# A planner that counts TensorE's products and keeps SyncE's transposes clear of instruction fetches

## The chip, the cores and the metric

The kernel runs on one core of one Trainium2 chip. The metric is the device time of one execution in microseconds (us); three timed executions are shown, and their median counts. One more execution was recorded by the hardware profiler, and has a time of its own.

The engines are called as the profile calls them: PE (TensorE, with PEld for its weight loads), DVE (VectorE), ACT (ScalarE), POOL (GpSimd) and SP (SyncE, which here issues nearly all DMAs). A q behind a name means the engine's sequencer, for instance while it issues a DMA.

## The reference

Two parts follow each other. The first is a linear attention with decay (RWKV6): batch 4, 8 heads, 768 tokens, head size 48.

```python
for t in range(S):
    cur = np.einsum('bhd,bhe->bhde', u[None] * kt, vt)
    y[:, :, t] = np.einsum('bhd,bhde->bhe', rt, state + cur)
    state = wt[:, :, :, None] * state + np.einsum('bhd,bhe->bhde', kt, vt)
...
h = x @ w_in
g = np.maximum(0.01 * h, h)
return g @ w_out
```

The second takes `y` as `x`, 3072 tokens of 384 values, through two dense layers with a leaky ReLU between them: 384 to 2048 and back to 384. Everything comes and goes as float32.

## The kernel before, in words

The 3072 tokens are cut into 24 chunks of 128, six to each batch element. A chunk goes through these steps:

- four loads of `w`, `k`, `r`, `v` into a tile `in` (L634, issued by SP; the first four chunks are loaded in pairs at L444);
- `lw`, the logarithm of the decays (L644, ACT), and its running sum `cum` on TensorE (L650, L653);
- two exponentials (L676, L680, ACT) and two products on DVE that give `rk`, the scaled `r` and `k` (L359);
- the transposed `rkT`. For the first 12 chunks TensorE transposes (L370) and DVE or ACT copies the result out; for chunks 12 to 23 (`RK_DMA = 12`) SP issues a transpose by DMA (L697);
- the scores on TensorE (L721), from chunk 8 on for two chunks in one step, the mask on DVE (L729), the state's sums (L739, L754) and the output `intra` (L765, L770);
- `y` (L432, DVE), with a bonus term that POOL and DVE make (L389 to L401), and its transpose into `xT`: on TensorE (L418) for the first 12 chunks, by DMA (L784) for chunks 12 to 23.

The dense layers run over blocks of one or two chunks: six of one, seven of two, four of one. "Up" multiplies `xT` by `w_in_b` (L828), ACT applies the leaky ReLU and writes `g` (L843), "down" multiplies `g` by `w_out_b` (L857); the result is copied (L868, L870) and stored (L874, SP). At the start TensorE runs 42 products of zeros (L894).

No scheduler orders this. The kernel calls no engine while it describes its work: `step` hands the class `Plan` each step with its possible engines and their costs, a priority, what it depends on, the tiles it reads and takes, and for a DMA a triple `wire` of wire time, size and latency. `Plan.order` then plays the steps through in time: whenever an engine is free, it takes from its ready steps the one with the smallest priority whose tiles are free. Attention steps have priorities of ten times the chunk's number, the dense layers 1000 and more, so the dense products fill TensorE wherever no attention step is ready. The order in which steps began there is the order in which the instructions are then written, for each engine; on the chip each engine works through its own list in order, and waits at a step whose data or tiles are not there.

For a DMA, the plan keeps SP busy for the step's cost, puts the wire time on one shared wire, and holds the data for landed the latency later. The costs for the transposes by DMA:

```python
TRK = (1.75, 64, 1.8)
TY = (0.65, 24, 1.8)
...
s_T = [step(
    {"SP": 0.6},
    lambda e: nc.sync.dma_start_transpose(
        out=rkT.t[:], in_=rk.t[:].rearrange("p a h d -> p (a h d)")),
    P0, deps=[s_r, s_k], reads=[rk], takes=[rkT], wire=TRK, late=0.5)]
```

Of the kernel before, what the change touches and what calls it, by code (L numbers as in the profile page):

```python
# [22 lines left out]
class Plan:  # L23
# [4 lines left out]
    SEEN = {"PE": 0.21, "DVE": 0.05, "ACT": 0.05, "POOL": 0.07, "SP": 0.05}  # L28

    def __init__(self, limits, slack_from, slack):  # L30
        self.steps, self.late, self.limits = [], [], limits
        self.slack_from, self.slack = slack_from, slack

    def add(self, engs, fn, pri, deps=(), reads=(), takes=(), wire=None, late=0.0):
        i = len(self.steps)
        self.late.append(late)
        self.steps.append([engs, fn, pri, {d for d in deps if d is not None}, tuple(reads), tuple(takes), wire])
        for b in (*reads, *takes):
            b.users.append(i)
        return i  # L40

    def order(self, pools):
        n = len(self.steps)
# [5 lines left out]
        bufs = {}  # L49
# [3 lines left out]
        remain = {k: len(b.users) for k, b in bufs.items()}  # L53
        free_tiles = {p: [(0.0, k) for k in range(len(t))] for p, t in pools.items()}
        in_use = {}
        ready_at = [0.0] * n
# [3 lines left out]
        events = []  # L60
        dma_free, flying = 0.0, []

        def offer(i, t):
# [9 lines left out]
        while events:  # L73
            now, kind, e, i = heapq.heappop(events)
# [12 lines left out]
            for e in self.ENGINES:  # L87
# [3 lines left out]
                while ready[e]:  # L91
                    pri, i = heapq.heappop(ready[e])
                    if self.start[i] is not None:
                        continue
                    want, ok = {}, True
                    for b in self.steps[i][5]:
                        if b.t is None:
                            want[b.pool] = want.get(b.pool, 0) + 1
                            if in_use.get(b.kind, 0) >= self.limits.get(b.kind, 99):
                                ok = False  # L100
                    for p, k in want.items():
                        if sum(f <= now + 1e-9 for f, _ in free_tiles[p]) < k:
                            ok = False
                    if ok:
                        chosen = i
                        break
                    held.append((pri, i))
# [16 lines left out]
                out.append(i)  # L124
                count += 1
                free[e] = now + d - (self.OVER[e] if d > 0.3 else 0.0)
                if wire is None:
# [20 lines left out]
        if count != n:  # L148
            raise RuntimeError(("stuck", count, n, [(self.steps[i][0], self.steps[i][2]) for i in range(n) if self.start[i] is None][:20]))
        return out  # L150

# [5 lines left out]
ROWS = (0.6, 8, 1.5)  # L157
TRK = (1.75, 64, 1.8)
TY = (0.65, 24, 1.8)


@with_exitstack
def kernel(
# [90 lines left out]
    with tc.manual_schedule():  # L254
# [55 lines left out]
        def weight_steps(q, which, pri):  # L310
# [13 lines left out]

            ld = step({"SP": 0.5}, load, pri, takes=[st], wire=WEIGHT)
            made = []
# [34 lines left out]
        def transposes(P0, rk, kind, s_d, rkTb, out_of, pri_k=0):  # L361

            tr = Buf("ps", "tr")

            def view(tr=tr):
                return tr.t[:].bitcast(BF16).rearrange("p (g t) -> p g t", t=128)

            def tpose(e):
                for g in range(NP):
                    nc.tensor.transpose(  # L370
                        view()[:, g, :], rk.t[:, kind, 2 * g : 2 * g + 2, :].rearrange("p h d -> p (h d)"), ident[:])

            def evac(e):
                if e == "DVE":
                    nc.vector.tensor_copy(out=out_of(), in_=view()[:, 0:NP, :])
                else:
                    nc.scalar.copy(out=out_of(), in_=view()[:, 0:NP, :])

            s_tr = step({"PE": 0.23}, tpose, P0, deps=[s_d], reads=[rk], takes=[tr])
            return step({"DVE": 0.42, "ACT": 0.59}, evac, P0, deps=[s_tr], reads=[tr], takes=[rkTb])  # L380
# [31 lines left out]
        def to_xt(P0, y, yp, s_ye, col_of):  # L412
            def yT():
                return yp.t[:].bitcast(BF16).rearrange("p (g t) -> p g t", t=128)

            def typose(e):
                for g in range(KT):
                    nc.tensor.transpose(  # L418
                        yT()[:, g, :], y.t[:].rearrange("p h d -> p (h d)")[:, g * 128 : (g + 1) * 128], ident[:])

            def xcopy(e):
                if e == "DVE":
                    nc.vector.tensor_copy(out=col_of(), in_=yT()[:, 0:KT, :])  # L423
                else:
                    nc.scalar.copy(out=col_of(), in_=yT()[:, 0:KT, :])
            s_yt = step({"PE": 0.18}, typose, P0 + 1, deps=[s_ye], reads=[y, yp])
            return step({"ACT": 0.48, "DVE": 0.36}, xcopy, P0 + 1, deps=[s_yt], reads=[yp])
# [9 lines left out]
        def pair(n):  # L437
# [23 lines left out]
            def cum(bank, mats):  # L461
                def go(e):
                    for j in range(2):
                        nc.tensor.matmul(
                            heads(bank.t), lhsT=mats[j][:], rhs=lw.t[:, j, :, 0:D], start=(j == 0), stop=(j == 1),
                            skip_group_check=True)
                return step({"PE": 0.33}, go, P0, deps=[s_ln], reads=[lw], takes=[bank])

# [15 lines left out]

            s_tot = step({"PE": 0.3}, total, P0 + 0.5, deps=[s_ln, s_cg], reads=[lw, cg])
            a_in = Buf("a")
# [41 lines left out]
            for js in range(2):  # L528
# [13 lines left out]

                s_sc = step({"PE": 0.42}, scores, P0 + 1, deps=s_T, reads=[rkT], takes=sc)
                m = Buf("m")
# [13 lines left out]
            def sums(e):  # L558
# [11 lines left out]
                {"PE": 0.4}, sums, P0 + 1, deps=[s_rk[1, 0], s_rk[1, 1], *s_vbs, s_sc],  # L570
                reads=[*rk, *vbs], takes=pp)
            sb, sx = Buf("sb"), Buf("s")
# [17 lines left out]
            def intra(e):  # L590
# [18 lines left out]
            s_y = step(  # L609
                {"PE": 1.2}, intra, P0 + 1, deps=[*s_ms, *s_vbs, *s_T, s_sb], reads=[*ms, *vbs, rkT, sb], takes=yps)  # L610
            for j in range(2):
# [8 lines left out]
        def single(n):  # L620
# [11 lines left out]
            for i, src in enumerate((w, k, r, v)):  # L632
                def load(e, src=src, i=i):
                    nc.sync.dma_start(out=part(i)(), in_=src[b, :, t0 : t0 + L, :].rearrange("h p d -> p h d"))  # L634
                lds.append(step(
                    {"SP": 0.5}, load, P0 + i * 0.1, takes=[slot], wire=LOAD,
                    deps=[firsts[n - AHEAD]] if n - AHEAD in firsts else []))
# [19 lines left out]

            s_cum = firsts[n] = step({"PE": 0.27}, cum, P0, deps=[s_ln], reads=[lw], takes=[cp])
            ci, ek = Buf("ci"), Buf("ps", "ek")
# [34 lines left out]
            else:  # L694
                s_T = [step(
                    {"SP": 0.6},
                    lambda e: nc.sync.dma_start_transpose(  # L697
                        out=rkT.t[:], in_=rk.t[:].rearrange("p a h d -> p (a h d)")),
                    P0, deps=[s_r, s_k], reads=[rk], takes=[rkT], wire=TRK, late=0.5)]
            vs, s_vs = bonus(P0, [slot], rv, kv, vv, ([rl], [kl], [vl]))  # L700
# [33 lines left out]
            if not last:  # L734
# [9 lines left out]

                s_pp = step({"PE": 0.17}, sums, P0 + 2, deps=[s_k, s_vb, s_sb], reads=[rk, vb], takes=[pp])

# [16 lines left out]
            def intra(e):  # L763
# [10 lines left out]
            s_y = step({"PE": 0.38}, intra, P0 + 1, deps=[*s_m, *s_T, s_vb, s_sb],  # L774
                reads=[m, vb, rkT] + ([] if first else [sb]), takes=[yp])
            y = Buf("y")
# [4 lines left out]
            else:  # L781
                xt_steps[n] = [step(
                    {"SP": 0.6},
                    lambda e: nc.sync.dma_start_transpose(  # L784
                        out=xT[:, :, col : col + L], in_=y.t[:].rearrange("p h d -> p (h d)")),
                    P0 + 1, deps=[s_ye], reads=[y], wire=TY, late=0.5)]
            yield
# [3 lines left out]
        for n in range(NCH):  # L791
# [3 lines left out]
            elif n % 2 == 0:  # L795
                two = [single(n), single(n + 1)]
                asked = [next(t) for t in two]
                if n >= JOIN:
                    (d0, t0, c0, f0), (d1, t1, c1, f1) = asked
                    s_sc = [step(  # L800
                        {"PE": 0.65}, lambda e, f0=f0, f1=f1: (f0(e), f1(e)), n * 10 + 1,
                        deps=[*d0, *d1], reads=[t0, t1], takes=[*c0, *c1])] * 2
                else:
                    s_sc = [
                        step({"PE": 0.42}, f, (n + i) * 10 + 1, deps=d, reads=[t], takes=c)
                        for i, (d, t, c, f) in enumerate(asked)]
# [7 lines left out]
        for nb, size in enumerate(blocks):  # L814
# [7 lines left out]
            for j in range(0, NJ, J):  # L822
                hp = Buf("ps", "hp")

                def up(e, hp=hp, j=j, J=J, N=N, c0=c0):
# [9 lines left out]
                s_up = step(  # L835
                    {"PE": J * KT * (N / 2400 + 0.0027)}, up, pri, takes=[hp],
                    deps=[s for ch in chs for s in xt_steps[ch]] + win_s[j * 128 // 512])
# [10 lines left out]
            for ch in chs:  # L848
                off = (ch - chs[0]) * L
                cols = [(0, 256), (256, DM)] if ch == NCH - 1 else [(0, DM)]  # L850
                for c_lo, c_hi in cols:
                    op = Buf("ps", "op")
                    s_dn = None
                    for q in range(4):
                        def down(e, op=op, g=g, q=q, off=off, c_lo=c_lo, c_hi=c_hi):
# [6 lines left out]
                            {"PE": 4 * ((c_hi - c_lo) / 2400 + 0.0025)}, down, pri,  # L862
                            deps=g_done[q * 4 : q * 4 + 4] + wout_s[q] + [s_dn], reads=[g], takes=[op])
                    o = Buf("o")

                    def ocopy(e, o=o, op=op, c_lo=c_lo, c_hi=c_hi):
# [5 lines left out]
                    step(  # L872
                        {"SP": 0.5},
                        lambda e, o=o, ch=ch, c_lo=c_lo, c_hi=c_hi: nc.sync.dma_start(  # L874
# [8 lines left out]
        step({"PE": 0.0}, lambda e: None, 1000.0, deps=[up_first[2]], reads=[warm])  # L883
        order = plan.order(pools)
        global PLAN
# [44 lines left out]
```

## Time and profile before

| what | us |
|---|---|
| timed runs | 183.87, 182.80, 183.69 |
| median | 183.69 |
| the profiled execution, its own time | 182.08 |
| its span, first to last instruction | 180.2 |
| PE busy in the span | 174.7 |
| DVE, ACT, POOL busy | 116.6, 110.7, 99.6 |
| `rkT<-rk` transposes by DMA: 12, median time from issue to landing | 4.1 |
| `xT<-y` transposes by DMA: 12, median time from issue to landing | 3.4 |

The span leaves out what lies around the first and the last instruction, 1.9 us here. Rows of the profile name an engine, a line of the kernel, and the tile written and the tiles read as out<-in. "PEld L828 <- DMA xT<-y: 0.3, 1, 0.3" in the list of waits means that weight loads of line 828 waited 0.3 us in total for a DMA into `xT`, once, 0.3 us at longest. In the DMA part, the queue named "instruction" carries the engines' own instructions, which are fetched while the kernel runs.

### The profile page before, as it was taken

What the parts mean: (1) busy time and instruction counts of PE and PEld (TensorE: products, weight loads), DVE (VectorE), ACT (ScalarE), POOL (GpSimd) and SP (SyncE); (2) the same over time, 40 slices, a digit from 0 to 9 for tenths busy, and PEclk for the clock granted to TensorE, in tenths of its full rate; (3) what the DMA queues carried; (4) which work ended last, traced back from release to release, by engine and by line L of the source; (5) the groups of instructions that cost most, each with busy time, mean ns of one, the idle gap of its engine ahead of it and who ended that gap; (6) DMA issues with size and microseconds to landing.
All of it is one profiled execution on the core that took longest, in us unless ns stands there. A gap on an engine that the chain in (4) does not pass through costs nothing.

```text
span 180.2 us, 5557 instructions
## 1 busy us (share of the span) xinstructions
PE 174.7 (97%) x2208; PEld 134.0 (74%) x2208; DVE 116.6 (65%) x241; ACT 110.7 (61%) x241; POOL 99.6 (55%) x141
## 2 busy tenths in 40 slices
PE   7999999999999999999999999999999999999993
PEld 4457887778778779787777687777687786778882
DVE  4389774369889799989489655686853484441111
ACT  2664868567978889857684168754286762535430
POOL 6297970376987898877837255654482655000000
PEclk9999999999999999999999999999999999999999
DMA  6999999899999999899999898999997992522102
GB/s 149 261 281 347 386 371 347 162 198 244 201 174 214 187 218 195 174 191 203 204 208 225 99 220 174 172 230 224 149 220 164 181 222 58 146 68 66 45 3 87
DMA packets 116524, 34.57 MB, mean 192 GB/s; under 512 B 109713, under 2 KB 114962, under 8 KB 116498
## 3 DMA queue, kind: packets, MB, share of 16 engines
q1 hardware_dynamic: 116496, 34.22, 94.3%
q8 instruction: 17, 0.28, 0.7%
q14 instruction: 9, 0.07, 0.1%
q10 hardware_dynamic: 2, 0.00, 0.0%
HBM read 25.17 MB, written 4.72 MB: 166 GB/s over the span
## 4 chain that ended last, share of the span: by engine, by line
PE 87%; ACT 3%; DMA 3%; DVE 2%; SPq 1%; issue 1%; DVEq 0%; ACTq 0%
PE ps L828 33%; PE ps L857 32%; PE ps L894 4%; PE ps L370 3%; DMA in<-in_w_dram 3%; PE ps L721 2%; PE ps L770 2%; PE ps L650 2%; PE ps L765 2%; PE ps L739 1%; PE ps L597 1%; SPq L634 1%; DVE m L549 1%; ACT g L843 1%; PE ps L418 1%
## 5 line engine op out<-in xcount | busy, mean ns | idle before, releaser
L828 PE MATMUL ps<-xT,w_in_b 128*128 128x128 bf16 (+1 forms) x816 | 75.9, 241 | 0.2
L843 ACT ACTIVATE g<-ps 128x512 bf16<-128x512 f32 x96 | 56.3, 597 | 32.0 <-PE ps L828 26.1
L857 PE MATMUL ps<-w_out_b,g 128*128 128x384 bf16 (+2 forms) x400 | 74.7, 319 | 0.1
L828 PEld LDWEIGHTS <-w_in_b 128*128 128x128 bf16 x816 | 60.0, 98 | 10.1 <-DVE xT L423 0.5
L857 PEld LDWEIGHTS <-g 128*128 128x128 bf16 x400 | 35.5, 97 | 15.8
L389 POOL TENSOR_TENSOR ru<-in,ub 128x384 f32<-128x384 f32 x24 | 24.0, 1000 | 21.0 <-DMA in<-in_k_dram 17.3
L359 DVE TENSOR_TENSOR rk<-in,ps 128x384 bf16<-128x384 f32 x48 | 25.1, 550 | 14.3 <-ACT ps L680 5.9
L393 POOL TENSOR_TENSOR ru<-ru,in 128x384 f32<-128x384 f32 x24 | 24.0, 999 | 8.9 <-DMA in<-in_r_dram 7.9
L729 DVE TENSOR_TENSOR m<-ps,maskb 128x512 bf16<-128x512 f32 x40 | 25.0, 682 | 4.3 <-PE ps L721 4.3
L401 POOL TENSOR_TENSOR vs<-in,dg 128x384 f32<-128x384 f32 x24 | 19.9, 830 | 8.7 <-DVE dg L397 8.6
L868 DVE COPY o<-ps 128x384 f32<-128x384 f32 (+2 forms) x16 | 8.5, 531 | 19.9 <-PE ps L857 14.3
L708 POOL TENSOR_TENSOR sb<-s,a 128x384 bf16<-128x384 f32 x18 | 14.9, 830 | 8.6 <-ACT a L671 8.5
L432 DVE TENSOR_TENSOR y<-ps,vs 128x384 bf16<-128x384 f32 x24 | 13.2, 552 | 5.1 <-PE ps L770 4.7
L397 DVE TENSOR_REDUCE dg<-ru 128x8 f32<-128x384 f32 x24 | 13.0, 547 | 4.0 <-POOL ru L393 4.0
L409 POOL CAST vb<-in 128x384 bf16<-128x384 f32 x24 | 12.0, 506 | 3.1 <-DMA in<-in_v_dram 2.2
L662 DVE TENSOR_TENSOR ci<-ps,lw 128x384 f32<-128x384 f32 x20 | 11.0, 552 | 3.6 <-PE ps L653 3.2
L644 ACT ACTIVATE lw<-in 128x384 bf16<-128x384 f32 x20 | 10.4, 522 | 2.0 <-DMA in<-in_w_dram 2.0
L676 ACT ACTIVATE ps<-ps 128x384 f32<-128x384 f32 x20 | 9.6, 480 | 2.9 <-DVE ci L662 2.6
L671 ACT ACTIVATE a<-ps 64x4 f32<-64x4 f32 x36 | 6.1, 169 | 8.1 <-DVE ci L662 7.0
L894 PE MATMUL ps<-zeros 128*128 128x256 bf16 (+1 forms) x42 | 9.0, 348 | 1.1 <-DVE zeros L257 1.1
L680 ACT ACTIVATE ps<-ci 128x384 f32<-128x384 f32 x20 | 9.8, 491 | 0.0
L754 DVE TENSOR_TENSOR s<-ps,sb 128x384 f32<-128x384 f32 x14 | 7.7, 550 | 2.1 <-PE ps L739 2.0
(78 smaller groups left out, 161.7 us busy)
## 6 DMA issues: line engine op xcount, KB each, us to landing
out_dram<-o SPq DMA_DIRECT2D x23, 192.0 KB, 3.3
in<-in_w_dram SPq DMA_DIRECT2D x20, 192.0 KB, 4.1
in<-in_k_dram SPq DMA_DIRECT2D x20, 192.0 KB, 4.0
in<-in_r_dram SPq DMA_DIRECT2D x20, 192.0 KB, 4.2
in<-in_v_dram SPq DMA_DIRECT2D x20, 192.0 KB, 4.0
in<-in_moe_w_in_dram SPq DMA_DIRECT2D x4, 768.0 KB, 9.5
in<-in_moe_w_out_dram SPq DMA_DIRECT2D x4, 768.0 KB, 12.7
in<-in_w_dram SPq DMA_DIRECT2D x2, 384.0 KB, 5.0
```

The costliest lines, as they stand in the source:

```text
L359: nc.vector.tensor_tensor(out=o, in0=x, in1=i, op=ALU.mult)
L389: lambda e: nc.gpsimd.tensor_tensor(out=ru.t[:], in0=kv(), in1=ubv, op=ALU.mult),
L393: lambda e: nc.gpsimd.tensor_tensor(out=ru.t[:], in0=ru.t[:], in1=rv(), op=ALU.mult),
L397: lambda e: nc.vector.tensor_reduce(out=dg.t[:], in_=ru.t[:], axis=AX.X, op=ALU.add),
L401: lambda e: nc.gpsimd.tensor_tensor(out=vs.t[:], in0=vv(), in1=dg.t[:].unsqueeze(2).to_broadcast([128, H, D]), op=ALU.mult),
L432: lambda e: nc.vector.tensor_tensor(out=y.t[:], in0=heads(yp.t), in1=vs.t[:], op=ALU.add),
L708: lambda e: nc.gpsimd.tensor_tensor(out=sb.t[:].rearrange("p g a d -> p (g a) d"), in0=s_in.t[:].rearrange("p g a d -> p (g a) d"), in1=a_ ...
L729: lambda e, par=par: nc.vector.tensor_tensor(out=m.t[:, par, :, :], in0=sc[par].t[:].rearrange("p (g t) -> p g t", g=NP), in1=maskb[:].uns ...
L828: nc.tensor.matmul(hp.t[:, a * N : (a + 1) * N], lhsT=w_in_b[:, t, (j + a) * 128 : (j + a + 1) * 128], rhs=xT[:, t, c0 : c0 + N], start=(a ...
L843: lambda e, hp=hp, g=g, j=j, J=J, N=N: nc.scalar.activation(out=g.t[:, j : j + J, 0:N], in_=hp.t[:, 0 : J * N].rearrange("p (a n) -> p a n ...
L857: nc.tensor.matmul(op.t[:, c_lo:c_hi], lhsT=g.t[:, j, off : off + 128], rhs=w_out_b[:, j, c_lo:c_hi], start=(j == 0), stop=(j == NJ - 1))
L894: nc.tensor.matmul(warm.t[:, 0:cols].rearrange("p (a n) -> p a n", n=256), lhsT=zeros[:, 0:128], rhs=zeros[:].unsqueeze(1).to_broadcast([1 ...
```

## The change

The planner gets a count of TensorE's products: each step on TensorE says how many it holds (`mm`), and the plan adds them up, starting from 36 for the zero products. It holds that an instruction fetch happens at product 866 and every 126.6 products from there. The order is made three times; from the second time on, the times of the fetches found in the run before are known, and a step marked `xbar` (the two transposes by DMA) may not begin on SP within 4.5 us ahead of a fetch. It is put off until the fetch begins, and SP takes another ready step. Besides, SP's costs are set anew: a load, a weight load and a store 0.57 instead of 0.5 us, a transpose 1.3 and 1.25 instead of 0.6, and the wire times and latencies of the transposes are made shorter. No instruction is added or taken away; the order of the instructions differs.

```diff
+    PIECE, FIRST_PIECE, ZEROS, CLEAR = 126.6, 866.0, 36, (0.0, 4.5)
...
-    def add(self, engs, fn, pri, deps=(), reads=(), takes=(), wire=None, late=0.0):
+        self.mm, self.xbar, self.fetches = [], [], []
+
+    def add(self, engs, fn, pri, deps=(), reads=(), takes=(), wire=None, late=0.0, mm=0, xbar=False):
         i = len(self.steps)
         self.late.append(late)
+        self.mm.append(mm)
+        self.xbar.append(xbar)
...
+        for b in bufs.values():
+            b.t, b.free_at = None, 0.0
...
+        products, piece, fetches = self.ZEROS, self.FIRST_PIECE, []
...
                     want, ok = {}, True
+                    until = max([f - self.CLEAR[0] for f in self.fetches if now < f - self.CLEAR[0] and f < now + self.CLEAR[1]], default=0.0)
+                    if self.xbar[i] and until > now + 1e-9:
+                        ok = False
+                        heapq.heappush(events, (until, 1, "SP", -1))
...
+                if e == "PE":
+                    products += self.mm[i]
+                    if products >= piece:
+                        fetches.append(now + d * (1 - (products - piece) / self.mm[i]))
+                        piece += self.PIECE
...
+        self.fetches = fetches
         return out
...
-TRK = (1.75, 64, 1.8)
-TY = (0.65, 24, 1.8)
+TRK = (1.25, 64, 1.2)
+TY = (0.47, 24, 1.0)
...
-                    {"SP": 0.5}, load, P0 + i * 0.1, takes=[slot], wire=LOAD,
+                    {"SP": 0.57}, load, P0 + i * 0.1, takes=[slot], wire=LOAD,
...
-                    {"SP": 0.6},
+                    {"SP": 1.3},
                     lambda e: nc.sync.dma_start_transpose(
                         out=rkT.t[:], in_=rk.t[:].rearrange("p a h d -> p (a h d)")),
-                    P0, deps=[s_r, s_k], reads=[rk], takes=[rkT], wire=TRK, late=0.5)]
+                    P0, deps=[s_r, s_k], reads=[rk], takes=[rkT], wire=TRK, late=0.5, xbar=True)]
...
-                    {"SP": 0.6},
+                    {"SP": 1.25},
                     lambda e: nc.sync.dma_start_transpose(
                         out=xT[:, :, col : col + L], in_=y.t[:].rearrange("p h d -> p (h d)")),
-                    P0 + 1, deps=[s_ye], reads=[y], wire=TY, late=0.5)]
+                    P0 + 1, deps=[s_ye], reads=[y], wire=TY, late=0.5, xbar=True)]
...
-        order = plan.order(pools)
+        for _ in range(3):
+            order = plan.order(pools)
```

The other places of the diff hand `mm` to each TensorE step, and 0.57 to the weight loads and the stores.

More of the change, by code (lines that the diff above doesn't have):

```diff
@@ L323, in load @@
                     )
-            ld = step({"SP": 0.5}, load, pri, takes=[st], wire=WEIGHT)
+            ld = step({"SP": 0.57}, load, pri, takes=[st], wire=WEIGHT)
             made = []
@@ L377, in evac @@
                     nc.scalar.copy(out=out_of(), in_=view()[:, 0:NP, :])
-            s_tr = step({"PE": 0.23}, tpose, P0, deps=[s_d], reads=[rk], takes=[tr])
+            s_tr = step({"PE": 0.23}, tpose, P0, deps=[s_d], reads=[rk], takes=[tr], mm=NP)
             return step({"DVE": 0.42, "ACT": 0.59}, evac, P0, deps=[s_tr], reads=[tr], takes=[rkTb])
@@ L425, in xcopy @@
                     nc.scalar.copy(out=col_of(), in_=yT()[:, 0:KT, :])
-            s_yt = step({"PE": 0.18}, typose, P0 + 1, deps=[s_ye], reads=[y, yp])
+            s_yt = step({"PE": 0.18}, typose, P0 + 1, deps=[s_ye], reads=[y, yp], mm=KT)
             return step({"ACT": 0.48, "DVE": 0.36}, xcopy, P0 + 1, deps=[s_yt], reads=[yp])
@@ L466, in go @@
                             skip_group_check=True)
-                return step({"PE": 0.33}, go, P0, deps=[s_ln], reads=[lw], takes=[bank])
+                return step({"PE": 0.33}, go, P0, deps=[s_ln], reads=[lw], takes=[bank], mm=2)
             c1, c0, cg, e0 = (Buf("ps", "cp2") for _ in range(4))
@@ L483, in total @@
                             rhs=ones[64:128, :], start=(j == 0), stop=(j == 1), skip_group_check=True)
-            s_tot = step({"PE": 0.3}, total, P0 + 0.5, deps=[s_ln, s_cg], reads=[lw, cg])
+            s_tot = step({"PE": 0.3}, total, P0 + 0.5, deps=[s_ln, s_cg], reads=[lw, cg], mm=2 * NP)
             a_in = Buf("a")
@@ L541, in scores @@
                                     start=True, stop=True, skip_group_check=True)
-                s_sc = step({"PE": 0.42}, scores, P0 + 1, deps=s_T, reads=[rkT], takes=sc)
+                s_sc = step({"PE": 0.42}, scores, P0 + 1, deps=s_T, reads=[rkT], takes=sc, mm=4 * NP)
                 m = Buf("m")
@@ L570, in pair @@
                 {"PE": 0.4}, sums, P0 + 1, deps=[s_rk[1, 0], s_rk[1, 1], *s_vbs, s_sc],
-                reads=[*rk, *vbs], takes=pp)
+                reads=[*rk, *vbs], takes=pp, mm=4 * NP)
             sb, sx = Buf("sb"), Buf("s")
@@ L609, in pair @@
             s_y = step(
-                {"PE": 1.2}, intra, P0 + 1, deps=[*s_ms, *s_vbs, *s_T, s_sb], reads=[*ms, *vbs, rkT, sb], takes=yps)
+                {"PE": 1.2}, intra, P0 + 1, deps=[*s_ms, *s_vbs, *s_T, s_sb], reads=[*ms, *vbs, rkT, sb], takes=yps, mm=8 * H + 2 * NP)
             for j in range(2):
@@ L656, in cum @@
                         rhs=ones[:], start=True, stop=True, skip_group_check=True)
-            s_cum = firsts[n] = step({"PE": 0.27}, cum, P0, deps=[s_ln], reads=[lw], takes=[cp])
+            s_cum = firsts[n] = step({"PE": 0.27}, cum, P0, deps=[s_ln], reads=[lw], takes=[cp], mm=1 if first else 1 + NP)
             ci, ek = Buf("ci"), Buf("ps", "ek")
@@ L743, in sums @@
                             start=True, stop=True, skip_group_check=True)
-                s_pp = step({"PE": 0.17}, sums, P0 + 2, deps=[s_k, s_vb, s_sb], reads=[rk, vb], takes=[pp])
+                s_pp = step({"PE": 0.17}, sums, P0 + 2, deps=[s_k, s_vb, s_sb], reads=[rk, vb], takes=[pp], mm=NP)
                 def state(e):
@@ L774, in single @@
             s_y = step({"PE": 0.38}, intra, P0 + 1, deps=[*s_m, *s_T, s_vb, s_sb],
-                reads=[m, vb, rkT] + ([] if first else [sb]), takes=[yp])
+                reads=[m, vb, rkT] + ([] if first else [sb]), takes=[yp], mm=H if first else H + NP)
             y = Buf("y")
@@ L801 @@
                         {"PE": 0.65}, lambda e, f0=f0, f1=f1: (f0(e), f1(e)), n * 10 + 1,
-                        deps=[*d0, *d1], reads=[t0, t1], takes=[*c0, *c1])] * 2
+                        deps=[*d0, *d1], reads=[t0, t1], takes=[*c0, *c1], mm=2 * H)] * 2
                 else:
                     s_sc = [
-                        step({"PE": 0.42}, f, (n + i) * 10 + 1, deps=d, reads=[t], takes=c)
+                        step({"PE": 0.42}, f, (n + i) * 10 + 1, deps=d, reads=[t], takes=c, mm=H)
                         for i, (d, t, c, f) in enumerate(asked)]
@@ L835 @@
                 s_up = step(
-                    {"PE": J * KT * (N / 2400 + 0.0027)}, up, pri, takes=[hp],
+                    {"PE": J * KT * (N / 2400 + 0.0027)}, up, pri, takes=[hp], mm=J * KT,
                     deps=[s for ch in chs for s in xt_steps[ch]] + win_s[j * 128 // 512])
@@ L862 @@
                             {"PE": 4 * ((c_hi - c_lo) / 2400 + 0.0025)}, down, pri,
-                            deps=g_done[q * 4 : q * 4 + 4] + wout_s[q] + [s_dn], reads=[g], takes=[op])
+                            deps=g_done[q * 4 : q * 4 + 4] + wout_s[q] + [s_dn], reads=[g], takes=[op], mm=NJ // 4)
                     o = Buf("o")
@@ L872 @@
                     step(
-                        {"SP": 0.5},
+                        {"SP": 0.57},
                         lambda e, o=o, ch=ch, c_lo=c_lo, c_hi=c_hi: nc.sync.dma_start(
```

## The prediction

> **What bounds the kernel now.** I read the page first, then TensorE's busy time by stage, then who TensorE waits for, and last SyncE's own timeline.
>
> ```profile
> span 180.2 us, 5557 instructions
> ...
> PE 174.7 (97%) x2208; PEld 134.0 (74%) x2208; DVE 116.6 (65%) x241; ACT 110.7 (61%) x241; POOL 99.6 (55%) x141
> ...
> PEclk9999999999999999999999999999999999999999
> ...
> q1 hardware_dynamic: 116496, 34.22, 94.3%
> q8 instruction: 17, 0.28, 0.7%
> ```
>
> TensorE is busy for 97% of the span, always at full clock. A busy PE need not be PE at its peak, so I looked at the starts of its products in the trace too: the 384-wide ones of L857 follow each other every 162 ns, the 256-wide of L828 every 109 ns, the 128-wide every 56 ns, almost everywhere. The last row is the fetching of instructions: 17 packets of 16 KB; 0.7% of 16 engines over 180.2 us is 20.2 us, 1.2 us each.
>
> ```profile
> 75.00:100.00 25.00, 25.00 (x287) 19.03 (x286) 20.35 (x41) 16.46 (x39) 17.75 (x23) 1.00 1.08 201
> 100.00:125.00 25.00, 24.86 (x271) 18.93 (x266) 17.18 (x32) 13.94 (x32) 12.94 (x16) 1.00 1.15 190
> 125.00:150.00 25.00, 25.00 (x260) 18.76 (x259) 15.42 (x29) 16.08 (x38) 13.97 (x17) 1.00 1.07 183
> 150.00:175.00 25.00, 25.00 (x315) 19.63 (x313) 6.43 (x12) 10.04 (x17) 1.39 (x3) 1.00 0.23 64
> ```
>
> Columns: stage and its length, then busy time of PE, PEld, DVE, ACT, POOL, clock, DMA share, GB/s. The transposes by DMA all lie here (78 to 162 us), and TensorE has no hole: 99.86 of 100 us.
>
> ```profile
> PE ps L894 <- DVE zeros L257: 1.1, 1, 1.1
> PE ps L597 <- issue: 0.4, 1, 0.4
> PE ps L537 <- DVE rkT L375: 0.2, 1, 0.2
> PE ps L597 <- DVE sb L575: 0.2, 1, 0.2
> ...
> PEld L828 <- DMA xT<-y: 0.3, 1, 0.3
> ```
>
> These are TensorE's waits (matmuls, and of its weight loads the one that names a transpose). One product in the run waited for a transpose, 0.3 us, at 152.40 us, where chunk 20's `xT` had landed at 152.35. The only other late start after 76 us is at 118.5 us, 0.33 us, behind an activation of `g`. So in this execution 0.6 us at most can be won where the change acts.
>
> ```profile
> 78.03 2.81 SPq L697 DMA_TRANSPOSE rkT<-rk  x1
> 80.95 0.52 SPq L634 DMA_DIRECT2D in<-in_v_dram  x1
> ...
> 112.00 1.79 SPq L697 DMA_TRANSPOSE rkT<-rk  x1
> 113.88 1.56 SPq L634 DMA_DIRECT2D in<-in_r_dram  x1
> ...
> 148.29 3.77 SPq L784 DMA_TRANSPOSE xT<-y  x2
> 152.17 1.24 SPq L697 DMA_TRANSPOSE rkT<-rk  x1
> ```
>
> SyncE's timeline: start, time taken by the issue. The trace has instruction packets starting at 78.91, 113.85 and 149.57 us. The transpose issued 0.9 us ahead of the first holds SyncE for 2.81 us against 1.24 for one with no fetch near; the load beside the second takes 1.56 against 0.52. So a fetch stretches whatever SyncE issues then. Ten of the 24 transposes begin within 4.5 us ahead of a fetch. Of `rkT<-rk`, the five such land 4.84 us after their issue in the mean (4.72, 4.95, 4.56, 5.12, 4.84), the six others with a record 3.89 (3.06 to 4.12): a fetch makes a transpose 0.95 us late.
>
> **The change, part by part.** No product, copy or DMA is added or taken away; the 42 zero products stay too. What changes is the order. In the instruction lists SyncE's first 65 DMAs are the same; the first to differ is chunk 12's `rkT` transpose, which three loads now overtake. TensorE's list is the same through 89.9 us of the trace, 1228 of 2207 products. Everything before that costs nothing.
>
> (1) Transposes held past a fetch. Gain: up to 0.95 us of landing for each of ten, off TensorE's path except for the 0.3 us at 152.40. Taken: 0.3, at most 0.6 with the wait behind `g`.
> (2) What goes ahead of them. A load costs SyncE 0.59 us in the median and meets the fetch instead: 1.56 at 113.88. Inputs are asked for many chunks ahead, so this is hidden by TensorE's up and down products; without that cover it would cost the stretch, about 1 us a fetch.
> (3) The truer costs. The plan held a `rkT` transpose to cost 0.6 of issue, 1.75 of wire and 1.8 us of latency, 4.15 us in all; now 1.3, 1.25 and 1.2, 3.75 us. Measured median: 4.1. For `xT` 3.05 becomes 2.72, measured 3.4. The plan puts a consumer on TensorE as soon as it believes the data there, and TensorE takes its list in order: a transpose that lands late stalls everything behind it. Here the change can lose.
>
> To price (3) I took each place where TensorE needs a transpose: the trace's start of the product less the landing is the margin before. Then I counted in both lists the products ahead of the consumer and of the last product that its data comes from (`cum` of the later chunk for scores, its `intra` for `xT`), turned the difference into time with the paces above, and added the change in SyncE's queue, 0.55 us for each DMA more ahead.
>
> Scores: chunks 12/13, margin 1.8, consumer 1.3 earlier, source unmoved: 0.5. Chunks 14/15, 2.4 (landing record missing; issue at 93.30 and the median): consumer 1.3 later, four more DMAs: about 1.5. Chunks 16/17, 1.0 (landed at 117.11, product at 118.07): consumer 31 products or 3.5 us earlier, source 1.7 earlier: -0.9, or 0.1 if it escapes its fetch. Chunks 18/19, 2.8: source 0.75 earlier, four DMAs more, and its issue near 122 us comes within 4 us of the fetch at 125.8: between 1.3 and 0.3. Chunks 20/21, 1.8: consumer 1.6 later, source 3.3 earlier, but held to the fetch's end near 140.6 us: 1.1. Chunks 22/23, 0.6: consumer 5.25 and source 5.1 earlier, and it loses the quiet in which it landed in 3.06: -0.5, or 0.8 with the two DMAs fewer ahead of it.
> `xT`: 12/13 from 2.7 to 1.2; 14/15 from 2.0 to between -0.4 and 1.2; 16/17 from 0.95 to between -0.1 and 1.5; 18/19 from 1.6 to between -1.1 and 0.3; chunk 20 from 0.05 to between -0.3 and 0.6; the rest over 2.
>
> The negative ends add up to 0.9 + 0.5 + 0.4 + 0.1 + 1.1 + 0.3 = 3.3 us, the other ends to nothing. Most places have both ends near zero, and a stall at one place gives SyncE time to catch up before the next; I take 0.5 of the 3.3.
>
> Sum: 182.08 us (the profiled execution's own time: span 180.2 and 1.9 around it), -0.3 and +0.5: 182.3. The three timed runs lie 0.7 to 1.8 us above the profiled one, the median 1.6. I keep that distance: 183.9.
>
> On instruction fetch the trace shows TensorE unbroken through all packets after 60 us. [...]
>
> **Rivals.** *Slower: landings past thin margins.* Should the transposes land as late as the negative ends have them, TensorE stalls up to 3.3 us in all, in front of L721 and L828: 183.7 + 3.3 - 0.3 = 186.7, near 186.2 if three quarters of it come. It decides from 1.8 us of stalls on. For it: the planned 3.75 us is below the measured 4.1, and the margins are below 1.3 us at most places. Against: the 1.3 us of issue now stands in the plan, so the queue drifts less than before.
> *Faster: the timed runs lose at fetches what the profiled one doesn't.* The 1.6 us between them has to be lost somewhere; if it is transposes made later by a fetch than the margins of 0.05 to 1.0 us allow, the change takes most of it away: 183.7 - 1.6 - 0.3 = 181.8. For it: three of the margins before are under 1 us, and a fetch adds 0.95. Against: nothing in this trace waits so, and the 1.6 us may be the runs' own.
> *It doesn't do what it says.* The plan counts products; fetches come at 59.6, 70.9, 78.9, 91.0, 101.6, 113.9 and 125.8 us, but with 102 to 147 products between them, up to 2 us off an even count. Then some transposes still meet one; others swap with a load that is stretched instead: 183.7, no change.
>
> **How the numbers follow.** The forecast (thin margins, little lost) 0.35; no effect 0.13; the slower rival 0.32; the faster 0.20. A difference under 1%, 1.8 us, is about what a measurement of this kernel can't tell from none; the first two cases are inside it (0.48), the slower rival lies outside on one side (0.32), the faster on the other by its greater part (0.20). Range: 182.0, near the faster rival, to 186.3, three quarters of the slower one; the forecast's own is 183.2 to 184.9.
>
> **What would show it.** Right: TensorE at 25.0 of 25 us in the first of the four stages, `rkT` transposes with a largest issue time near 1.7 instead of 2.81 us and landings of 3.9 to 4.2, loads of 1.5 to 2.2 us beside the fetches; a few waits "PEld L721 <- DMA rkT" or "PEld L828 <- DMA xT" of 0.1 to 0.5 us after 110 us, near chunks 16 to 19 first. Wrong on the slower side: these sum to 2 us and more, or a wait on DVE or ACT in their place. Wrong on the faster side: timed runs that come down to the profiled one.

## The result, and the profile after

| | before | changed |
|---|---|---|
| timed executions, median, us | 183.57 (six, 182.80 to 183.92) | 184.97 (six, 184.41 to 185.41) |
| the profiled execution, its own time | 182.08 | 184.93 |
| its span | 180.2 | 183.2 |

The ratio of the times is 1.008, with a 95% interval of 1.0053 to 1.0106: slower by 1.4 us, which is under the 1% that the prediction drew as its line, and clear of no change. The six of before hold the three shown above. Medians here and below are of executions in the faster of two states, which leaves out one execution each of wires_only, latency_only and later_landing_no_hold.

The stages of the changed kernel, as they were read before (stage and length; busy time of PE, PEld, DVE, ACT, POOL; clock, DMA share, GB/s):

```profile
75.00:100.00 25.00, 25.00 (x281) 19.10 (x279) 19.70 (x41) 16.86 (x40) 19.14 (x24) 1.00 1.07 202
100.00:125.00 25.00, 23.80 (x262) 17.70 (x261) 16.30 (x31) 14.90 (x36) 11.44 (x15) 1.00 0.94 176
125.00:150.00 25.00, 23.86 (x229) 17.15 (x227) 13.44 (x26) 15.11 (x33) 14.80 (x19) 1.00 1.00 189
150.00:175.00 25.00, 25.00 (x323) 19.81 (x322) 7.87 (x14) 9.91 (x17) 0.00 (x0) 1.00 0.25 68
```

TensorE, which had 99.86 of these 100 us, now has holes of 1.2 and 1.1 us in the two middle stages. Who made them stands in the waits of the matmuls and of the weight loads:

```profile
PE ps L847 <- DMA xT<-y: 1.3, 2, 0.8
...
PE ps L758 <- POOL vs L420: 0.7, 1, 0.7
...
PE ps L669 <- ACT lw L663: 0.3, 1, 0.3
...
PEld L847 <- DMA xT<-y: 1.2, 1, 1.2
...
PEld L740 <- DMA rkT<-rk: 0.2, 1, 0.2
```

(19 lines lie ahead of each old line: L847 is the old L828, L740 the old L721.) The starts of the products in the trace say how long each one came after the pace of its form (a weight load's wait is not its product's: before, at 152.4 us, one waited 0.3 us and its product came 0.1 late): up products waited for `xT` 0.51 us at 102.1, 1.00 at 126.9 and 0.15 at 140.5; the state's sums (L758) waited 0.23 at 109.5 and 0.85 at 113.1 for data made from input loads; a running sum (L669) 0.43 at 131.9 for `lw`, made from the load of `w`; scores 0.20 at 149.1 for `rkT`. Together 3.4 us after 75 us; before it was 0.3, of which 0.2 at 118.8 us behind an activation and 0.1 at 152.4 us for `xT`.

Did the change do what it says? The instruction packets of the changed kernel start at 79.4, 90.5, 103.8, 114.8, 128.6, 142.7 and 153.8 us. No `rkT` transpose is issued within 2.6 us ahead of one, and of all 24 transposes one is, an `xT` at 153.3 us; before there were eight. Within the 4.5 us that the plan keeps clear there still are eight (the prediction counted ten before): the plan's times and the chip's drift apart.

```profile
L716 SPq DMA_TRANSPOSE rkT<-rk x12: 1237/1286/1750, 81.4 to 149.4; - x12
```

This line, from what the profile says of L716, has the shortest, median and longest issue in ns: the longest is 1.75 where it was 2.81 us. Landings fell to between 3.02 and 3.92 us, 3.51 in the mean, which is less than the 3.89 that the prediction read as free of fetches; why, no run shows. So the transposes did become faster, and the kernel slower. SyncE's timeline shows the other side:

```profile
96.95 1.28 SPq L716 DMA_TRANSPOSE rkT<-rk  x1
98.33 2.51 SPq L803 DMA_TRANSPOSE xT<-y  x2
100.94 1.25 SPq L716 DMA_TRANSPOSE rkT<-rk  x1
102.28 0.53 SPq L653 DMA_DIRECT2D in<-in_v_dram  x1
102.86 0.64 SPq L653 DMA_DIRECT2D in<-in_w_dram  x1
103.59 1.75 SPq L893 DMA_DIRECT2D out_dram<-o  x1
105.43 0.39 SPq L653 DMA_DIRECT2D in<-in_k_dram  x1
```

There is no free moment: four transposes in a row, the fetch at 103.8 meets a store instead, which takes 1.75 us to issue where the median store takes 0.53, and only then comes chunk 18's load of `k`, from which the chain of waits runs through POOL to the 0.85 us at 113.1. After 60 us SyncE's issues of transposes take 32.7 us in all instead of 38.7, those of loads and stores 57.3 instead of 50.3.

### The profile page after: what moved, and what is told of

Its sections match the earlier page's. It is cut to its first block, busy times and chain, and to the rows that moved or that the text cites. A ratio compares the mean times of both kernels' runs of the same rounds, so it can differ in the third digit from the quotient of the medians.

```text
span 183.2 us, 5569 instructions
## 1 busy us (share of the span) xinstructions
PE 175.5 (96%) x2208; PEld 133.9 (73%) x2208; DVE 115.1 (63%) x239; ACT 112.2 (61%) x243; POOL 98.9 (54%) x141
## 4 chain that ended last, share of the span: by engine, by line
PE 76%; DMA 9%; SPq 7%; POOL 3%; DVE 2%; issue 1%; ACT 1%; DVEq 0%; POOLq 0%
PE ps L876 31%; PE ps L847 30%; DMA in<-in_moe_w_in_dram 5%; SPq L463 4%; PE ps L740 3%; DMA in<-in_w_dram 2%; PE ps L389 2%; PE ps L789 2%; DMA in<-in_k_dram 2%; PE ps L669 2%; PE ps L784 1%; PE ps L758 1%; DVE m L748 1%; PE ps L437 1%; SPq L334 1%
## 5 line engine op out<-in xcount | busy, mean ns | idle before, releaser
L847 PE MATMUL ps<-xT,w_in_b 128*128 128x128 bf16 (+1 forms) x816 | 76.7, 241 | 1.4 <-DMA xT<-y 1.3
L876 PE MATMUL ps<-w_out_b,g 128*128 128x384 bf16 (+2 forms) x400 | 75.9, 319 | 0.0
L847 PEld LDWEIGHTS <-w_in_b 128*128 128x128 bf16 x816 | 60.2, 98 | 12.0 <-DMA xT<-y 1.2
L887 DVE COPY o<-ps 128x384 f32<-128x384 f32 (+2 forms) x14 | 7.4, 527 | 24.3 <-PE ps L876 14.7
L889 ACT COPY o<-ps 128x384 f32<-128x384 f32 x11 | 5.2, 477 | 7.4 <-PE ps L876 7.3
```

Of the source, the lines that this page charges most:

```text
L847: nc.tensor.matmul(hp.t[:, a * N : (a + 1) * N], lhsT=w_in_b[:, t, (j + a) * 128 : (j + a + 1) * 128], rhs=xT[:, t, c0 : c0 + N], start=(a ...
L876: nc.tensor.matmul(op.t[:, c_lo:c_hi], lhsT=g.t[:, j, off : off + 128], rhs=w_out_b[:, j, c_lo:c_hi], start=(j == 0), stop=(j == NJ - 1))
```

## The experiments

Twelve kernels ran, each beside the kernel before on the same chip. Four theories were held. A: the hold costs, since it bunches transposes and lets loads come late. B: the shorter latencies cost, because they leave consumers no margin. C: any new order of a full queue costs by chance. D, formed after the first eight: the wire time costs. It is the plan's account of how much the DMA path carries; the change cuts it by 12 times 0.5 and 12 times 0.18, 8.2 us, and the plan then asks for more than the path delivers.

All are the changed kernel with constants altered; half_stores, further down, keeps them and has smaller stores. The last column is how far landings trail the times that the kernel's own plan has for them (trace less plan, median of the DMAs that the plan starts in 15 us): near 70 us, nearly all before the change acts, and near 145 us.

| kernel | hold | SyncE's costs | wire time | latency | median, us | ratio to before | trails by, us |
|---|---|---|---|---|---|---|---|
| before | no | old | old | old | 182.9 to 183.6 | 1 | 1.6, then 0.7 |
| changed | yes | new | short | short | 184.97 | 1.008 (1.0053 to 1.0106) | 1.3, then 4.5 |
| hold_only | yes | old | old | old | 186.24 | 1.015 (1.0076 to 1.0225) | 3.1, then 1.7 |
| hold_issue | yes | new | old | old | 185.85 | 1.0117 (1.0044 to 1.019) | 1.9, then 1.2 |
| issue_only | no | new | old | old | 182.65 | 0.9976 (0.9948 to 1.0005) | 1.9, then 2.0 |
| latency_only | no | old | old | short | 182.81 | 1.0007 (0.9968 to 1.0045) | 1.6, then 1.7 |
| issue_short_latency | no | new | old | short | 183.90 | 1.0023 (0.999 to 1.0056) | 1.9, then 2.4 |
| wire_time_only | no | old | short | old | 188.53 | 1.029 (1.0247 to 1.0334) | 1.4, then 6.9 |
| wires_only | no | old | short | short | 188.78 | 1.0349 (1.0277 to 1.0421) | 1.5, then 7.1 |
| costs_no_hold | no | new | short | short | 185.83 | 1.0137 (1.0084 to 1.019) | 2.0, then 4.5 |
| later_landing | yes | new | short | +1.0 | 186.29 | 1.0144 (1.0102 to 1.0187) | 1.3, then 3.8 |
| later_landing_no_hold | no | new | short | +1.0 | 187.51 | 1.0216 (1.0164 to 1.0269) | 2.2, then 5.8 |
| shifted_holds | yes, elsewhere | new | short | short | 186.61 | 1.0183 (1.0126 to 1.0241) | 1.6, then 5.3 |

**The parts one by one.** hold_only and its expectation:

```diff
-TRK = (1.25, 64, 1.2)
-TY = (0.47, 24, 1.0)
+TRK = (1.75, 64, 1.8)
+TY = (0.65, 24, 1.8)
...      SyncE: 0.57, 1.3 and 1.25 back to 0.5, 0.6 and 0.6
```

> The costs of before (0.5, 0.6; wires 1.75 and 0.65), but transposes held 4.5 us ahead of a fetch. Theory A (the hold itself costs: SyncE's queue is never idle from 75 to 148 us, and the loads that pass the held transposes, and the transposes bunched behind the fetch, come late): 1.4 us or more over before, with TensorE waiting for input loads and xT. Theory B (the shorter wires and latencies cost: consumers are placed before the data can land): no more than 0.4 us over before. Theory C (any new order of this full list costs about a microsecond by chance): 0.5 to 2 us over before, at places that have nothing to do with transposes.

wires_only keeps the new TRK and TY, takes the old costs, and sets `CLEAR` to (0.0, 0.0), which holds nothing:

> Only the transposes' shorter wires and latencies (1.25/1.2 and 0.47/1.0), no hold, SyncE's costs as before. Theory A: within 0.4 us of before. Theory B: 1 us or more over before, with waits for rkT and xT named in TensorE's waits. Theory C: 0.5 to 2 us over before.

issue_only (TRK and TY as before, no hold) and costs_no_hold (only `CLEAR` set to zero):

> Only SyncE's costs as traced (0.57, 1.3, 1.25), no hold, the longer wires. The plan now knows of a fuller queue. Theory A: within 0.5 us of before, or better, since nothing is held. Theory B: likewise within 0.5 us, since the landing stays cautious. Theory C: 0.5 to 2 us over before.

> All new costs, no hold: the changed kernel without its hold. Theory A: within 0.5 us of before (183.6), so 1 us or more under the changed kernel. Theory B: at the changed kernel's 185.0, with waits for rkT and xT. Theory C: anywhere from 184 to 185.5.

The hold alone cost 3.2 us, wires and latencies alone 5.7, SyncE's truer costs nothing that can be told (0.4 us less). So A and B both seemed to have a part. The changed kernel was no slower than the same without the hold (1.008 against 1.0137, intervals that just overlap), though alone the hold costs.

That cost stands in the plan already. Played through with no chip, the plan of before ends at 179.8 us, hold_only's at 183.8 and hold_issue's at 184.0, with TensorE idle for 4.4 and 4.6 us after 75 us in the plan itself (0.4 in before's). The plans of the changed kernel and of costs_no_hold both end at 179.9: with the short wire times the hold costs the plan nothing. The plan's end is no forecast to the microsecond (issue_only's lies at 181.2, and its time did not rise), but it could have been asked before any run.

**Which of the wires' two numbers.** hold_issue is issue_only with the hold; later_landing and its twin without hold take the changed kernel with `TRK = (1.25, 64, 2.2)` and `TY = (0.47, 24, 2.0)`:

> The hold and SyncE's costs as traced, with the longer wires and latencies of before: the changed kernel with its landing made cautious again. Theory A (the hold costs: alone it took 186.2 against 183.1): 1.4 us or more over before. Theory B (the shorter wires and latencies cost: alone they took 189.1): within 0.5 us of before. If both act, between 0.5 and 2 us over.

> The changed kernel with 1.0 us more of latency for both transposes (2.2 and 2.0), all else kept, the hold too. Theory B: the waits for xT and rkT go, and the time comes down to 183.6 or less. Theory A: it stays at 185 or goes up, with waits for input loads.

> SyncE's costs as traced, the shorter wires, 1.0 us more of latency, no hold. Theory B and theory A both: within 0.5 us of before, and 182.6 or less if the truer issue times are worth what they were alone (0.4 us). At 185 both are wrong, and any new order of a full SyncE queue costs by chance.

hold_issue came 2.2 us over before, as theory A had it. Together with issue_only and costs_no_hold it shows that, with SyncE's new costs, the hold without the short wire times costs 1.2%, the short wire times without the hold 1.4%, both together 0.8%, and neither nothing: the changed kernel's time comes back only when both are taken out.

Theory B failed here: a microsecond more of latency than the changed kernel has did not bring the time down (1.0144 against 1.008 with the hold, 1.0216 against 1.0137 without, intervals that overlap). A fails too: later_landing_no_hold has no hold and is slow. In every one of these profiles TensorE waited for `xT` or for `lw`, at other places each time. What those with the short wire times share is the last column of the table: landings trail the plan by ever more, however cautious the latency. That was theory D, and the next two kernels split the pair:

```diff
-TRK = (1.25, 64, 1.2)
-TY = (0.47, 24, 1.0)
+TRK = (1.25, 64, 1.8)      # wire_time_only
+TY = (0.47, 24, 1.8)
+TRK = (1.75, 64, 1.2)      # latency_only
+TY = (0.65, 24, 1.0)
```

> Only the wire times shortened (1.25 and 0.47), latencies 1.8 and SyncE's costs as before, no hold. Theory D (the wire time is the plan's account of a DMA path that is full until 150 us; shortened by 12 times 0.5 and 12 times 0.18, 8.2 us, the plan asks for more than the path carries, and every landing falls ever later behind the plan): landings 4 us or more behind the plan at 145 us, where the kernel before has 0.7, and 1.5 us or more over before. Theory B (the shorter latency leaves too little margin): within 0.5 us of before. Theory C (any new order costs by chance): 0.5 to 3 us over.

> Only the latencies shortened (1.2 and 1.0), wire times 1.75 and 0.65 and SyncE's costs as before, no hold. Theory D: landings less than 2.5 us behind the plan at 145 us, no growth along the run, and within 0.6 us of before. Theory B: 1 us or more over before, with waits for rkT and xT. Theory C: 0.5 to 3 us over.

Middle stages of wire_time_only, then of latency_only:

```profile
100.00:125.00 25.00, 22.12 (x236) 16.78 (x234) 15.21 (x29) 14.06 (x34) 14.12 (x18) 1.00 1.06 184
125.00:150.00 25.00, 22.05 (x215) 15.75 (x213) 12.39 (x24) 13.97 (x33) 13.89 (x18) 1.00 1.15 182
```

```profile
100.00:125.00 25.00, 25.00 (x262) 19.21 (x261) 15.85 (x30) 15.43 (x36) 12.13 (x15) 1.00 0.93 184
125.00:150.00 25.00, 25.00 (x257) 18.52 (x256) 14.68 (x27) 15.52 (x36) 14.26 (x18) 1.00 1.20 196
```

The shorter wire time alone makes 5.8 us of holes and 2.9%; the shorter latency alone leaves TensorE whole in these stages (its one longer stall, 0.8 us for `xT`, comes at 152.5 us) and the time where it was. Theory D came out as expected in both, B and C in neither. Chance would not sort the kernels without the hold so, either: the four with short wire times are 1.4 to 3.5% slower, the three with the old ones lie within 0.3% of before.

The rate itself can be read. The first DMA of SyncE that the change can move is its 66th. From there to the 131st, 65 DMAs of nearly the same mix, the chip took 67.4 us in before and 68.0 to 70.0 us in every other kernel, whatever the plan. The plans with the old wire times give them 66.9 to 68.2 us, at most 1.9 less than the chip then took; those with the short ones give them 61.8 to 65.3, which is 3.8 to 8.2 too few.

**The hold's place.** shifted_holds has `FIRST_PIECE = 929.3`, half a piece later:

> The changed kernel with the counted fetches set half a piece (63.3 products) later, so that transposes are held clear of places where no fetch comes. If keeping clear of the true fetches is worth anything, several rkT transposes show issue times over 2 us or landings near 4.8 us again and the time is 0.5 us or more above the changed kernel's 185.0. If the places don't matter, only the order that comes out: 185.0, give or take 0.8.

It came 1.6 us above the changed kernel's median (the ratios 1.0183 and 1.008 have intervals apart), and transposes met fetches again: two of `rkT`, 1.6 and 0.7 us ahead of a fetch, took 2.34 and 2.33 us to issue (a third took 2.00 with no fetch within 4.9 us), two landed 5.37 and 4.84 us after it. Around the fetch at 115.5 us the `xT` transposes of chunks 14/15 took 1.98 and 1.91 us, the first landed 4.98 us after its issue, and the up products behind them came 1.95 us late. But the plan of shifted_holds ends 2.8 us after the changed kernel's by itself (182.7 against 179.9), and it charges nothing for a fetch. So the order alone may account for the 1.6 us, and whether the true places are worth holding clear is not shown.

**Whether the DMA engines are what is full.** half_stores:

```diff
-                            out=rows[ch][:, c_lo:c_hi], in_=o.t[:, c_lo:c_hi]),
+                            out=rows[ch][0:64, c_lo:c_hi], in_=o.t[0:64, c_lo:c_hi]),
```

> The changed kernel, same order, but each store writes 64 of its 128 rows (the other half of the result is left out). SyncE issues as many DMAs as before; the DMA engines get about 18 times 0.3 us less to do before 150 us. Theory D: landings 2 us or less behind the plan at 145 us instead of 4.5, and a time of 183.0 to 184.0. If SyncE's issuing is what is full, or the margins alone count: 185.0, lag as before.

The time stayed at 185.05 us (1.0121, 1.0061 to 1.0182), and landings trail by 3.2 instead of 4.5 us: a miss for theory D, and no clean one. The packets of the main queue filled 87.3% of 16 engines over 182.5 us instead of 89.0% over 183.2, 3.7 us less over all 25 stores, or 0.15 us a store: half of what the expectation took off. Whether the path is full at the engines or at SyncE's issuing (its longest idle stretch between 78 and 146 us is under 0.2 us, in both kernels) stays open.

**A version that beats both.** issue_short_latency was the attempt:

> A version that might beat both: SyncE's costs as traced and the shorter latencies, but the wire times of before and no hold. Theory D: no growing lag, 182.2 to 183.2, at or under SyncE's costs alone (182.65). Theory B: 184 or more. Theory C: 184 to 186.

At 1.0023 it is no better than before, and its 183.90 us lies 0.7 us above the stretch that theory D gave; issue_only is not better beyond its interval either. No kernel here beats the one before clearly.

## Why the prediction was right or wrong

The time lies in the range and inside the line of 1%, and on the side that the point of 183.9 leaned to; it is 1.1 us above the point, and just above the forecast's own 183.2 to 184.9. That it came so near is in good part luck, as the fifth point below says. By its steps:

*No TensorE stall at a fetch, little to win (step 1).* Right. The two waits of before in that stretch are gone, and no product comes late at a fetch itself (the store that one stretches at 103.8 us does hold one up at 113.1). Of the 0.3 us that the step took as its gain only 0.1 was TensorE's: the weight load waited 0.3, its product came 0.1 late. `rkT` transposes land 0.8 us sooner in the mean (4.32 before, all with a record; 3.51 now), and in hold_issue, with old wires, 3.74 bought nothing.

*Loads take the fetch and are hidden (step 2).* Half right, and mis-sized: loads and stores took over the stretch (7.0 us more), but they were priced at nothing, and the waits for what is made from them came to 0.23 + 0.85 + 0.43 = 1.5 us of the 3.4. "Asked for many chunks ahead" was argued from the code; SyncE's queue, with no gap of 0.2 us between its issues from 78 to 146 us before, was the row to ask.

*Thin margins (step 3).* The right rows of TensorE, L828 and L721, in the wrong proportion. 0.5 us was taken of 3.3; 1.9 came: 1.7 at `xT` and 0.2 at scores, near the 2 us that the prediction named as the sign of being wrong on the slower side, and the wait for ACT's `lw` is another of its signs. The margin given to chunks 12/13 (1.2) was a stall of 0.5, 16/17 (between -0.1 and 1.5) one of 1.0, 18/19 (between -1.1 and 0.3) one of 0.15; the worst bet, scores of 16/17 at -0.9, did not stall.

*Its reason.* Wrong. The step set issue plus wire plus latency, 3.75 us, against a measured landing of 4.1, as if one transpose stood alone. In the plan each one also queues for the wire behind other DMAs: from start to landing an `rkT` transpose takes 5.65 us there in the median before and 4.55 in the changed plan, against 4.1 and 3.5 on the chip. So single transposes land sooner than planned in both kernels, and what trails is the queue. latency_only shortens that same sum by 0.6 and 0.8 us and costs nothing; wire_time_only shortens it by 0.5 and 0.18 us and costs 2.9%. In the plan a wire time is charged to every DMA behind it, a latency to its own consumer only. That the sum was made of two kinds of number is what the step did not see.

*The profiled execution against the median.* The 1.6 us between them was carried over, and was not a property of the kernel: the changed kernel's profile (184.93) lies at its median (184.97), and executions of before spread from 181.83 to 184.40 us over all experiments. From profile to profile the change costs 2.85 us, from median to median 1.4. The sum against the profile, 182.3, was thus 2.6 us low, and the carried distance hid most of that by luck. Part of the distance arises before the change acts: the first up products of chunk 6, behind the same instructions in all, begin at 62.2 us before, 62.1 in the changed kernel, 63.1 in issue_only and 63.5 in hold_only. The rest is not settled.

*The rivals.* The slower one named landings past thin margins, with 1.8 us of stalls as the point where it decides: stalls were 3.4 us in the profile, 1.9 of them at transposes, and the median yet moved by 1.4 only. So its mechanism was at work as much as the forecast's. (Three quarters of its 3.3 us give 185.9, not 186.2: the 0.3 was left out there; nothing turns on it.) The faster one is out: timed executions did not come down. "It doesn't do what it says" is out in its time, and by the 1.75 us; that other DMAs are stretched instead did come.

## What to carry to other kernels

In a planner's cost of a transfer, the part that occupies the shared path and the part that only delays its own data have to be measured apart. Here single transposes that land 0.8 us sooner were worth nothing while the queue was full, and an understated occupied part let the landings fall further behind along the run, from 1.4 to 6.9 us in wire_time_only. To see it, subtract the planned landing from the traced one along the run: a growing difference is a rate that the plan has wrong. Then compare the ends of the plans themselves: hold_only trails its plan no more at the end than at the start, and is slow all the same, since its plan is longer. And before a moved transfer is priced at zero, look at whether its queue has any idle time to be late in.

## What the runs showed of the hardware that was not expected

In wires_only a wait of TensorE was followed by a stretch at a lower clock. Stages of that kernel:

```profile
120.00:125.00 5.00, 5.00 (x48) 3.86 (x46) 3.15 (x8) 4.15 (x11) 2.79 (x4) 1.00 1.23 232
125.00:130.00 5.00, 3.24 (x30) 1.99 (x27) 2.85 (x5) 2.56 (x5) 2.08 (x3) 1.00 0.95 140
130.00:135.00 5.00, 4.48 (x40) 2.87 (x41) 1.85 (x3) 1.20 (x4) 3.21 (x4) 0.66 1.34 211
```

TensorE was idle for 2.2 us, from 128.3 to 130.5 us, waiting for `rkT`; the granted clock was 0.66 in the mean of the 5 us from 130 us on, and 384-wide products followed each other there every 320 ns instead of 162. In hold_issue an idle stretch of 2.0 us was followed by a clock of 0.91 in the mean from 130 to 135 us and of 0.75 from 135 to 140. After one of 2.5 us in later_landing_no_hold and one of 1.8 us in shifted_holds the clock stayed at 1.0, so the length of the wait alone does not decide; what does, no run shows. By an estimate from these means (0.34 of 5 us; 0.09 and 0.25 of 5 us) the lower clock cost 1.7 us in each of the two; hold_issue's executions lie apart in the same way, 184.03 and 184.96 us with a mean clock of 1.0, 186.75 and 186.77 with 0.991. So part of what hold_issue and wires_only (0.988 to 0.990) took longer is the clock's.
